# A written-out order for every engine, and a different first batch, in an attention and gated feed-forward kernel

## The chip, the cores and the metric

The kernel runs on one core of one Trainium2 chip. The metric is the device time of one execution in microseconds (us). Most executions of one kernel agree within 0.3 to 1%; a run more than 1.5% above the fastest of its kernel is called slow, and ratios use the other, fast, runs alone. "Span" is the length of the one execution that the profiler recorded; it is some 2 us shorter than that execution's device time. The engines are PE (TensorE, matmuls; PEld is its weight load), DVE (VectorE), ACT (ScalarE), POOL (GpSimd) and SP (SyncE, which here only issues transfers).

## The reference

```python
# x: (4, 12416, 128), inducing: (32, 128), w_gate, w_val: (128, 1536), w_out: (1536, 128); all fp32
def mab(q, kv):
    s = scale * (q @ kv.transpose(0, 2, 1))
    s = s - s.max(-1, keepdims=True)
    a = np.exp(s)
    a /= a.sum(-1, keepdims=True) + 1e-09
    return a @ kv
h = mab(I, x)                       # 32 inducing points look at the 12416 tokens of a batch
return mab(x, h)                    # the tokens look at the 32 results
...
gate = 1.0 / (1.0 + np.exp(-(x @ w_gate)))
val = x @ w_val
return (gate * val @ w_out)         # on all 49664 tokens
```

`h` of a batch needs all of that batch, and every output of the batch needs `h`. So before the first output there is a **prologue** (all of batch 0 loaded, cast, transposed, scored and summed); later batches do this beside the outputs of the batch ahead of them.

## The kernel before

Each batch has 97 tiles of 128 tokens: six quads of 16 tiles, the last with a 17th. A **unit** is 512 tokens; a batch has 24 and a tail of one tile, 24.25 in all. As the attention output is a weighted sum of 32 rows of `h`, the kernel folds `h` into the weights (`hw` is `h @ [w_gate w_val]`, 32 rows), so gate and value of a token are products of its 32 attention weights with `hw`. Matmuls write into the PSUM memory, where buffers are few. Per unit there are six gate products (PSUM buffer `g`, two of them), six tanh on ACT (sigmoid is 0.5 + 0.5 tanh(x/2)), twelve value products (PSUM buffer `v`, three), eleven of which DVE multiplies with the gate, one of which ACT copies out for GpSimd to multiply, 48 output matmuls into `acc`, and one copy of `acc` to SBUF by ACT.

```python
# one gate pair, one value block and its multiply (cut)
o = op("PE", 0.216, key + 0.1 + 0.05 * k, gd + ([g0] if g0 else []), mode="R", rg=k,
       need=[] if g0 else ["G"], emit=em, name=f"G{b}.{u}.{lo}.{k}")
a = act(w, key, gs + tg.old, give=[(g0, "G")], name=f"T{b}.{u}.{lo}",
        emit=lambda o, g0=g0, tg=tg, w=w: ACT.activation(out=tg.t[:, 0:w], in_=psl("G", g0)[:, 0:w], func=AF.Tanh, scale=0.5))
...
key = 1000 + LEAD + m // 2 + (0.05 if m % 2 == 0 else 0.3)
v = op("PE", 0.216, key, gd, mode="R", rg=rg, need=["V"], emit=em, name=f"V{b}.{u}.{q}")
d = dve(512, key, [v, a] + ub.old, give=[(v, "V")], name=f"D{b}.{u}.{q}",
        emit=lambda o, v=v, tg=tg, t0=t0, ub=ub: DVE.scalar_tensor_tensor(
            out=ub.t[:], in0=tg.t[:, t0 : t0 + TOK], scalar=1.0, in1=psl("V", v)[:], op0=ALU.add, op1=ALU.mult))
```

The operations carry a key, a duration, their dependences and the PSUM buffer that they need or give back. A list scheduler orders them while the program is built: each engine takes, among its pending operations in the order of the keys, the one that is ready first.

```python
def schedule(ops, pools, window=120):
    ...
    pend = {e: sorted((o for o in ops if o.eng == e), key=lambda o: o.key) for e in engs}
    ...
            for o in pend[e][: (60 if e in ("SP", "POOL") else window)]:
                ...
                r = max(r, d.start if d.eng == e == "PE" else d.end + (d.tail if d.eng != e or e in ("SP", "POOL") else 0.0))
                ...
                if cand is None or r < cand[0] - 1e-9:
                    cand = (r, o)
```

On the chip that order is then fixed: each engine executes its own list from first to last and waits at an entry whose inputs or buffers are not there, even if a later entry could go. The prologue loads the inducing points first, through GpSimd's own queue, then x through three staging buffers, and casts half of each quad on DVE and half on GpSimd; ACT casts two of the weights.

```python
ind_ld = op("POOL", 0.9, -10, tail=2.0, emit=lambda o: POOL.dma_start(ind16[:], inducing), name="ld ind")
...
c0 = op("DVE", 8 * P / 960 * 0.6 + 0.065, key + 3, [lm] + buf.old, name=f"cast{i}a",
        emit=lambda o: DVE.tensor_copy(out=buf.t[:, 0:h, :], in_=sg.t[:, 0:h, :]))
c1 = op("POOL", 8 * P / 960 + 0.3, key + 3, [lm] + buf.old, name=f"cast{i}b",
        emit=lambda o: POOL.tensor_copy(out=buf.t[:, h:QS, :], in_=sg.t[:, h:QS, :]))
...
wl["wo"] = op("POOL", 3.0, 40, [landed(ld, max(0.1, arrive[0] - 0.6 * 9))], name="wo2", ...)   # out weights times 0.5
```

The softmax here doesn't subtract the row's maximum and nothing guards it: scores larger than these inputs give would overflow.

Of the kernel before, what the change touches and what calls it, by code (L numbers as in the profile page):

```python
# [18 lines left out]
SEM = 0.085  # L19
DRAIN = 0.166  # L20
SWITCH = 0.1
RSTEP = 0.005
TSTEP = 1.12
LEAD = 3


class Op:


    def __init__(self, eng, dur, key, deps=(), mode="F", rg=0, tail=0.0, need=(), give=(), emit=None, name=""):  # L30
        self.eng, self.dur, self.key = eng, dur, key
        self.deps = [d for d in deps if d is not None]
        self.mode, self.rg, self.tail = mode, rg, tail
        self.need, self.give, self.emit, self.name = list(need), list(give), emit, name
        self.start = self.end = None
        self.slot = None
        self.strict = False


def schedule(ops, pools, window=120):  # L40
    engs = sorted({o.eng for o in ops})
    pend = {e: sorted((o for o in ops if o.eng == e), key=lambda o: o.key) for e in engs}
    free = {e: 0.0 for e in engs}
    mode, rgb, peend = None, [0.0] * 4, 0.0
    slotfree = {p: {i: 0.0 for i in range(n)} for p, n in pools.items()}
    inf = 1e18
    order = []
    while len(order) < len(ops):
        best = None
        for e in engs:  # L50
            cand, t0 = None, free[e]
            stop = False
            for o in pend[e][: (60 if e in ("SP", "POOL") else window)]:
                if stop:
                    break
                stop = o.strict
                r = t0
                for d in o.deps:
                    if d.start is None:
                        r = inf  # L60
                        break
                    r = max(r, d.start if d.eng == e == "PE" else d.end + (d.tail if d.eng != e or e in ("SP", "POOL") else 0.0))
                if r >= inf:
                    continue
                for p in o.need:
                    r = max(r, min(slotfree[p].values()))
                if r >= inf:
                    continue
                if e == "PE":
                    if o.mode == "R":  # L70
                        r = max(r, rgb[o.rg]) if mode == "R" else max(r, peend + SWITCH)
                    else:
                        r = max(r, peend + (SWITCH if mode != o.mode else 0.0))
                if cand is None or r < cand[0] - 1e-9:
                    cand = (r, o)
                if r <= t0 + 1e-9:
                    break
            if cand and (best is None or cand[0] < best[0]):
                best = (cand[0], e, cand[1])
        if best is None:  # L80
            raise RuntimeError("no op can go: " + str({e: [o.name for o in pend[e][:3]] for e in engs}))
        r, e, o = best
        o.start, o.end = r, r + o.dur
        if e == "PE":
            if o.mode == "R":
                if mode != "R":
                    rgb = [0.0] * 4
                rgb[o.rg] = o.end
                free[e] = r + RSTEP
            else:  # L90
                free[e] = o.end
            peend = max(peend, o.end)
            mode = o.mode
        else:
            free[e] = o.end
        pend[e].remove(o)
        order.append(o)
        for p in o.need:
            i = min(slotfree[p], key=lambda k: slotfree[p][k])
            slotfree[p][i] = inf  # L100
            o.slot = i
        for s, p in o.give:
            slotfree[p][s.slot] = o.end + o.tail
    order.sort(key=lambda o: o.start)
    return order
# [13 lines left out]


class Buf:
    def __init__(self, t, old, users):
        self.t, self.old, self.users = t, old, users
# [10 lines left out]
def kernel(  # L134
# [19 lines left out]
    psum = ctx.enter_context(tc.tile_pool(name="ps", bufs=1, space=bass.MemoryType.PSUM))  # L154

# [9 lines left out]
    PSG = [ps(f"g{i}", [P, 2 * TOK]) for i in range(2)]  # L165
    PSV = [ps(f"v{i}", [P, TOK]) for i in range(3)]
    PSA = [ps("acc", [P, TOK])]
    POOLS = {"G": 2, "V": 3, "A": 1}
# [3 lines left out]
    ones = sb("ones", [P, P], F32)  # L172
    ind16 = sb("ind16", [M, C])
# [21 lines left out]
    N4 = [sb(f"n4{r}", [P, 4, 4, M]) for r in range(4)]  # L195
    A2PR = ring("a2p", 2, [P, 640])
    A2R = ring("a2r", 3, [P, 4, 640])
    dram = ctx.enter_context(tc.tile_pool(name="dr", bufs=1, space=bass.MemoryType.DRAM))
    DRR = Ring([dram.tile([P, 640], F16, name=f"dr{i}", tag=f"dr{i}") for i in range(3)])
    TGA = sb("tga", [P, 12 * 2 * TOK])  # L200
    TGR = Ring([TGA[:, 2 * TOK * i : 2 * TOK * (i + 1)] for i in range(12)])
    UR = ring("u", 18, [P, TOK])
    VSR = ring("vs", 2, [P, TOK], F32)
    PTR = ring("pt", 2, [P, TOK], F32)
    OSR = ring("os", 4, [P, 4, C], F32)

    XS = xT[1][:].bitcast(F32)
    XSR = Ring([XS[:, QS * P * i : QS * P * (i + 1)].rearrange("p (s c) -> p s c", c=P) for i in range(3)])
    XS1 = sb("xs1", [P, C], F32)
    WS = [TGA[:].bitcast(F32)[:, F * (1 + i) : F * (2 + i)] for i in range(3)]  # L210
# [3 lines left out]
    def chain(ins, eng):  # L214
        prev = last.get(eng)
        if prev is not None:
            tc.add_manual_dep(
                ins.ins,
                prev.name,
                mybir.DependencyInfo(mybir.DependencyClass.NoSync, mybir.DependencyReason.DATA),  # L220
                reason="order",
            )
        last[eng] = ins.ins
        return ins

    class Eng:
# [3 lines left out]
        def __getattr__(self, f):  # L230
            fn = getattr(self.e, f)

            def go(*a, **k):
                return chain(fn(*a, **k), self.name)  # L234

            return go
# [5 lines left out]
    _affine_eye(nc, ident[:], [[-1, P]])  # L242
    for r in range(4):
        _affine_eye(nc, I4[32 * r : 32 * r + 32, :], [[-1, M]])
    nc.vector.memset(ones[:], 1.0)
    for q in range(2):
        nc.vector.memset(sacc[q][:], 0.0)
        nc.gpsimd.memset(ER.tiles[q][:], 0.0)
# [3 lines left out]
    def op(eng, dur, key, deps=(), **k):  # L252
        tails = {"PE": DRAIN + SEM, "ACT": 0.12 + SEM, "DVE": 0.085 + SEM, "POOL": 0.25, "SP": 2.6}
        k.setdefault("tail", tails[eng])
        o = Op(eng, dur, key, deps, **k)
        ops.append(o)
        return o

    def act(n, key, deps=(), **k):
        return op("ACT", n * 0.857e-3 + 0.03, key, deps, **k)  # L260

    def dve(n, key, deps=(), **k):
        return op("DVE", n / 960 + 0.065, key, deps, **k)

    def psl(kind, o):
        return {"G": PSG, "V": PSV, "A": PSA}[kind][o.slot]

    xv = [x[b].rearrange("(p s) c -> p s c", p=P) for b in range(B)]
    ov = [out[b * N : (b + 1) * N].rearrange("(p s) c -> p s c", p=P) for b in range(B)]


    units = [(b, u) for b in range(B) for u in range(NB + 1)]
    gfirst, vfirst, wsteps, gap = {}, {}, {}, {}
    ng = nv = 0
    lastw = -10
    for b, u in units:
        gfirst[b, u] = ng
        vfirst[b, u] = LEAD + nv / 2
        ng += 2 if u == NB else 6
        nv += 3 if u == NB else 12  # L280
        st = max(int(vfirst[b, u]) + 3, lastw + 2)
        ws = [st] * 12 if u == NB else [st, st, st + 1, st + 1, st + 1, st + 2, st + 2, st + 3, st + 3, st + 3, st + 4, st + 4]
        wsteps[b, u] = ws
        lastw = ws[-1]
        gap[b, u] = lastw + 1

    steps = {}

    def at_step(n):

        n = min(max(int(n), 0), ng - 1)
        return [steps[n]] if n in steps else []


    wl = {}
    ind_ld = op("POOL", 0.9, -10, tail=2.0, emit=lambda o: POOL.dma_start(ind16[:], inducing), name="ld ind")
    ind_t = op("PE", 0.1, -9, [ind_ld], need=["V"], name="indT",
               emit=lambda o: PE.transpose(psl("V", o)[:].bitcast(F16)[:, 0:M], ind16[:], ident[0:M, 0:M]))
    ind_c = dve(32, -9, [ind_t], give=[(ind_t, "V")], name="indTc",
                emit=lambda o: DVE.tensor_copy(out=indT[:], in_=psl("V", ind_t)[:].bitcast(F16)[:, 0:M]))  # L300
    BW = 330e3
    xload = {}

    def load_quad(b, i, key, after=()):
        buf = XR.take()
        ns = QS + 1 if i == NQ - 1 else QS
        o = op("POOL", 0.6, key, list(buf.old) + list(after), tail=8.0, name=f"ld x{b}.{i}",
               emit=lambda o: POOL.dma_start(buf.t[:, 0:ns, :], xv[b][:, i * QS : i * QS + ns, :]))
# [525 lines left out]
```

## Time and profile before

| | before |
|---|---|
| median of its first three runs (range) | 778.87 us (776.96 to 779.79) |
| first gate matmul, first output copied out of `acc` | 53.5 us, 67.6 us |
| from output 5 to 30, 30 to 55, 55 to 80 (a batch each, 24.25 units) | 183.1, 181.0, 182.3 us |
| from output 80 to 98 (18 units, nothing of a next batch beside them) | 124.7 us |

### The profile page before, as it was taken

To read this page: it belongs to the slowest core of one execution; us is meant where nothing else is said; L and a number is where in the kernel's file an instruction comes from. 1 tells how busy PE (TensorE), PEld (TensorE's weight loads), DVE (VectorE), ACT (ScalarE), POOL (GpSimd) and SP (SyncE) were. 2 spreads that over 40 slices of the span, in tenths; PEclk is the share of its full clock that TensorE was granted. 3 is DMA by queue.
4 is the path that set the end of the run, shared out by engine and by line. 5 is a ranking of instruction groups with operands and counts; after the bars stand their busy time and mean duration, and the time that the engine had idled before them with its cause. 6 is when DMAs were issued, how large, how long until landed. Compare 5 with 4: busy or idle time off the path is not lost.

```text
span 778.2 us, 20470 instructions
## 1 busy us (share of the span) xinstructions
PE 684.4 (88%) x7851; PEld 369.7 (48%) x7851; DVE 692.4 (89%) x1157; ACT 698.7 (90%) x883; POOL 339.2 (44%) x448
## 2 busy tenths in 40 slices
PE   3579988899899988989899988999989999999997
PEld 2324544445454544545445444444545454445444
DVE  2548998999899999999899999999899999999997
ACT  2449998999999999999899999999899989999996
POOL 3424453534525445445444436344354445445332
PEclk9758999999999999999999999999999999999999
DMA  9772449565421329675422236522231213222211
GB/s 349 184 124 67 108 88 180 116 129 132 95 73 53 90 82 158 130 164 115 122 70 66 69 96 118 124 71 77 60 104 36 79 64 74 81 72 59 79 43 45
DMA packets 113186, 78.64 MB, mean 101 GB/s; under 512 B 80576, under 2 KB 97472, under 8 KB 112320
## 3 DMA queue, kind: packets, MB, share of 16 engines
q1 hardware_dynamic: 110448, 67.80, 32.8%
q0 software_dynamic: 2640, 9.54, 7.9%
q8 instruction: 61, 1.00, 0.6%
q14 instruction: 37, 0.30, 0.1%
HBM read 39.99 MB, written 28.57 MB: 88 GB/s over the span
## 4 chain that ended last, share of the span: by engine, by line
PE 50%; issue 16%; POOL 12%; ACT 10%; DVE 9%; DMA 2%; ACTq 0%; POOLq 0%; DVEq 0%
PE acc L234 26%; PE v L234 20%; DVE u L234 7%; ACT tga L234 6%; POOL u L234 4%; POOL pt L234 4%; PE g L234 4%; ACT os L234 2%; POOL tree L234 2%; POOL a2n L234 2%; DMA a<-eT 2%; DVE x L234 1%; DMA ind<-in_inducing_dram 1%; ACT xT L234 1%; ACT eT L234 0%
## 5 line engine op out<-in xcount | busy, mean ns | idle before, releaser
L234 DVE SCALAR_TENSOR_TENSOR u<-tga,v 128x512 f16<-128x512 f16 x1068 | 663.4, 682 | 44.7 <-PE v L234 32.0
L234 ACT ACTIVATE tga<-g 128x1024 f16<-128x1024 f32 x584 | 579.8, 1039 | 31.9 <-PE v L234 8.1
L234 PE MATMUL v<-a2r,hw 32*128 32x512 f16 (+1 forms) x1200 | 338.9, 379 | 21.0 <-DVE u L234 20.6
L234 PEld LDWEIGHTS <-u 128*128 128x128 f16 x4656 | 266.4, 99 | 183.0 <-issue 181.7
L234 PE MATMUL acc<-wo,u 128*128 128x128 f16 x4656 | 349.9, 222 | 0.7 <-ACT os L234 0.7
L234 POOL TENSOR_TENSOR pt<-tga,vs 128x512 f32<-128x512 f16 x96 | 111.8, 1164 | 354.3 <-ACT vs L234 346.9
L234 PE MATMUL g<-a2r,hw 32*128 32x512 f16 (+1 forms) x1200 | 230.2, 383 | 32.7 <-ACT tga L234 32.0
L234 PEld LDWEIGHTS <-hw 32*128 32x128 f16 x2400 | 70.4, 91 | 139.6 <-issue 87.0
L234 POOL TENSOR_TENSOR u<-pt,vs 128x512 f16<-128x512 f32 x96 | 121.7, 1267 | 7.6
L234 ACT COPY vs<-v 128x512 f32<-128x512 f32 x96 | 56.5, 588 | 8.4 <-PE v L234 7.3
L234 ACT COPY os<-acc 128x512 f32<-128x512 f32 (+1 forms) x100 | 58.2, 582 | 3.3 <-PE acc L234 3.3
L234 POOL TENSOR_TENSOR a2n<-e2t,rc 128x128 f16<-128x128 f16 x96 | 37.3, 481 | 18.4 <-DVE rc L234 18.4
L234 ACT COPY xT<-v 128x1024 f16<-128x1024 f16 (+1 forms) x7 | 6.3, 906 | 23.1 <-PE v L234 23.1
L234 POOL TENSOR_TENSOR tree<-tree 128x64 f32<-128x64 f32 (+4 forms) x69 | 23.7, 344 | 5.4
L234 POOL DMA_DIRECT2D x<-in_x_dram x18 | 10.5, 585 | 27.6 <-PE v L234 13.4
L234 ACT ACTIVATE e<-g 128x512 f16<-128x512 f32 (+1 forms) x24 | 15.5, 649 | 4.3 <-PE g L234 4.3
L234 ACT ACTIVATE eT<-g 128x512 f16<-128x512 f32 (+1 forms) x28 | 15.6, 563 | 3.2 <-PE g L234 3.2
L234 PE MATMUL g<-xT,indT 128*32 128x512 f16 (+1 forms) x112 | 13.2, 388 | 3.9 <-ACT xT L234 2.9
L234 PEld LDWEIGHTS <-hT 128*32 128x32 f16 (+1 forms) x136 | 6.5, 95 | 20.4 <-issue 18.2
L234 PEld LDWEIGHTS <-a 128*32 128x32 f16 x388 | 7.3, 98 | 18.6 <-issue 9.5
L234 POOL TENSOR_TENSOR tree<-e2t 128x256 f32<-128x256 f16 (+1 forms) x23 | 15.9, 690 | 0.4 <-DMA e2t<-e 0.4
L234 PE MATMUL v<-ident,x 128*128 128x128 f16 x97 | 10.5, 281 | 3.9 <-DVE x L234 2.4
(59 smaller groups left out, 141.5 us busy)
## 6 DMA issues: line engine op xcount, KB each, us to landing
out_dram<-os SPq DMA_DIRECT2D x96, 256.0 KB, 2.0
a2r<-dr SPq DMA_DIRECT2D x92, 128.0 KB, 2.8
x<-in_x_dram POOLq DMA_DIRECT2D x15, 512.0 KB, 5.7
xT<-in_x_dram SPq DMA_DIRECT2D x6, 1024.0 KB, 9.0
dr<-a2p SPq DMA_DIRECT2D x19, 128.0 KB, 2.0
x<-in_x_dram POOLq DMA_DIRECT2D x3, 544.0 KB, 5.3
xT<-x SPq DMA_TRANSPOSE x75, 2.5
tga<-in_moe_w_gate_dram SPq DMA_DIRECT2D x1, 768.0 KB, 10.3
```

Of the source, the lines that this page charges most:

```text
L234: return chain(fn(*a, **k), self.name)
```

## The change

Its intent is to take the order out of the scheduler's hands: the order of all five engines for the whole program is written down, 5,627 names, and the build only plays it. With it came a different first batch: six fp32 loads at once into buffers that are idle then, casts on GpSimd, the last quad's scores token-major in three parts, summed straight into the accumulator.

```diff
-LEAD = 3
+COPIES = (3,)
+ORDER = {
+    "PE": """
+        xt0.8 xt0.0 indT xt1.8 sa0.0 xt1.0 ap0 xt2.8 sa0.1 xt2.0 hp0.0 ap1 xt3.0 sa0.2 hp0.1 xt3.8 ap2 xt4.0 hp0.2 sa0.3
...   (PE, ACT, DVE, POOL: some 390 lines of names cut)
+    "SP": """
+        lx0.0 lx1.0 lx2.0 lx3.0 lx4.0 lx5.8 lx5.0 lx5.13 lwg lind lwo lwv xd1.0.2 xd1.0.0 xd1.0.3 xd1.0.1 et0.1 xd1.1.0
...
-def schedule(ops, pools, window=120):
-    engs = sorted({o.eng for o in ops})
-    pend = {e: sorted((o for o in ops if o.eng == e), key=lambda o: o.key) for e in engs}
...
+def play(ops, order, pools):
+    by = {o.name: o for o in ops}
+    todo = {e: [by[n] for n in names] for e, names in order.items()}
...
+                    o.slot = len(u) % n          # PSUM buffers are taken in turn
...
-    ind_ld = op("POOL", 0.9, -10, tail=2.0, emit=lambda o: POOL.dma_start(ind16[:], inducing), name="ld ind")
+    ld = load(ind32[:], inducing, 40000, "lind")                     # by SP's queue, tenth in its order
+    ind_b = dve(64, [ld], "ind16", lambda o: DVE.tensor_copy(out=ind16[:], in_=ind32[:]))
...
-    XSR = Ring([XS[:, QS * P * i : QS * P * (i + 1)].rearrange("p (s c) -> p s c", c=P) for i in range(3)])
+    XS = [f32v(TGA)[:, 0 : QS * P]] + [f32v(xT[1])[:, QS * P * i : QS * P * (i + 1)] for i in range(3)]
+    XS += [f32v(UA)[:, 0 : QS * P], f32v(UA)[:, QS * P : (2 * QS + 1) * P]]
...
+    for i in range(NQ - 1):
+        load0(i, ((0, QS, ((0, 8, "POOL"), (8, 16, "POOL"))),))
+        xt_pe(i, ((0, 8), (8, 16)))
+        stage1_pro(i)
+    i = NQ - 1
+    load0(i, ((0, 8, ((0, 4, "POOL"), (4, 8, "DVE"))), (8, 13, ((8, 10, "POOL"), (10, 13, "DVE"))),
+              (13, 17, ((13, 15, "DVE"), (15, 17, "ACT")))))
+    groups = ((0, 8), (8, 13), (13, 17))
+    stage1_last(i, groups, xt_pe(i, groups))
...
-        wl[nm] = act(F, 25 + n, ..., name=nm, emit=lambda o, n=n, dst=dst: ACT.copy(out=dst, in_=WS[n]))
+        wl[nm] = op("POOL", 1.7, [ld], nm, lambda o, n=n, dst=dst: POOL.tensor_copy(out=dst, in_=WS[n]))
```

The counts of tanh, products, copies and output matmuls of a unit stay. In the names, `lx`/`cx` load and cast x of batch 0, `lind` and `lwg lwv lwo` load inducing points and weights, `G T V D C P W E` are gate matmuls, tanh, value matmuls, DVE products, ACT copies, GpSimd products, output matmuls and the copy of `acc`; `ld` and `xd` load and transpose x of later batches, `sa` is a first score, `et tr mu` the row sums of second scores.

## The prediction

> **What bounds the kernel now.** I read the page's shares and slices first, then a table by stage, then the timeline of the first 60 us, then the waits of the long middle.
>
> The page's first part gives busy time by engine:
>
> ```profile
> PE 684.4 (88%) x7851; PEld 369.7 (48%) x7851; DVE 692.4 (89%) x1157; ACT 698.7 (90%) x883; POOL 339.2 (44%) x448
> ```
>
> Three engines stand within 14 us of each other, so there is no single bound, and freeing one of them is worth little. The table by stage tells more (columns: stretch, its length, then busy us of PE, PEld, DVE, ACT and POOL with counts, granted clock, DMA share, GB/s):
>
> ```profile
> 80.00:700.00 620.00, 563.00 (x6546) 303.71 (x6546) 577.96 (x970) 587.25 (x740) 280.28 (x367) 0.99 0.41 96
> 700.00:765.00 65.00, 60.48 (x680) 31.84 (x679) 63.92 (x106) 62.66 (x76) 25.90 (x28) 1.00 0.18 58
> ```
>
> From 80 to 700 us ACT is busy 94.7% and DVE 93.2%; from 700, where no work for a next batch is mixed in, DVE reaches 98.3%. Of one unit (512 tokens, 12 column blocks) ACT does six tanh, one copy of v and one copy of the output. DVE does eleven products. In runs without a gap a tanh starts every 0.92 us (a pair took 1.94, one alone 1.02), a copy every 0.49, a product every 0.60. So a unit asks 6 x 0.92 + 2 x 0.49 = 6.5 us of ACT and 11 x 0.60 = 6.6 of DVE. A batch adds about 10.4 us of ACT: six first scores at about 0.7, six second ones at 0.55, three folds at 0.92. Over 24 units that is 0.43, so 6.93 for ACT. What is achieved: from 100 to 700 the view of the tanh alone counts 489, which is 81.5 units, 7.36 us each; in the three busier batches (100 to 600: 404 tanh) it is 7.43. In the last batch the copies of v stand 6.85 us apart. So the loss against the floor is about 0.5 us a unit in three batches, and about 0.25 in the last.
>
> What ended the gaps there (waits from 80 to 765 us: total us, times, longest):
>
> ```profile
> PE g L234 <- ACT tga L234: 31.1, 51, 0.7
> DVE u L234 <- PE v L234: 27.3, 79, 1.3
> PE v L234 <- DVE u L234: 23.7, 103, 1.1
> ```
>
> PE waits for a g buffer that ACT empties, DVE for a v, PE for a v buffer that DVE empties: a ring of three busy engines around two g and three v buffers. Only order can mend that, not a cheaper instruction.
>
> The prologue, from the timeline (start, length, engine, what, idle time before it and who ended it):
>
> ```profile
> 3.98 0.71 POOL L234 DMA_DIRECT2D ind<-in_inducing_dram  x1
> ...
> 9.78 0.20 PE L234 MATMUL v<-ident,ind 32*128 32x32 f16 x1 [9.78 <-DMA ind<-in_inducing_dram]
> ...
> 24.36 6.36 DVE L234 CAST x<-xT 128x1024 f16<-128x1024 f32 x1
> ...
> 45.15 0.29 DVE L234 TENSOR_TENSOR hT<-v,rsb 128x128 f16<-128x128 f32 x1
> ...
> 53.50 1.03 PE L234 MATMUL g<-a2r,hw 32*128 32x512 f16 x4 [0.52 <-DVE a2r L234]
> ```
>
> The inducing points arrive at 9.8, one DVE cast takes 6.36 us instead of its usual 0.68, the first h is ready at 45.4, the first gate matmul is at 53.5. That is 7% of the span with ACT mostly idle.
>
> **What the Trainium skill says.** (1) "DMA: Bandwidth & Descriptors", section "Two DMAs through the same engine are not ordered": within one queue of one engine, descriptors start in order. The trace agrees. The DMA issues of the first 60 us:
>
> ```profile
> tga<-in_moe_w_gate_dram SPq DMA_DIRECT2D x1, 768.0 KB, 10.3
> tga<-in_moe_w_val_dram SPq DMA_DIRECT2D x1, 768.0 KB, 11.5
> xs<-in_x_dram SPq DMA_DIRECT2D x1, 64.0 KB, 9.1
> ```
>
> The 64 KB load, issued at 2.1 behind three loads of 1 MB, landed only at 11.2, just after the third of those (whose cast starts at 11.09); the weights at 13.1 and 15.0. (2) "SBUF — State Buffer", section "Who interferes with whom": a DVE copy in a two-port mode and a GpSimd instruction shut each other out. The 6.36 us cast agrees: GpSimd had two casts and the scaling of wo (4.12 us) running from 24.04 to 30.16. (3) "TensorE: Matmul & The Clock Gate", Part 1: the clock halves when the engine has been idle and returns after some 3.4 us of activity. The trace agrees: eight transposes took 1.03 us when cold at 14.4, sixteen took 1.07 from 18.2.
>
> **The change part by part.**
>
> Prologue. *Removed:* the waits of loads four to six for a staging buffer, DVE's half of the casts for five quads, the ACT casts of the weights (2 x 1.48), the expansion copies on GpSimd. *Added:* casts on GpSimd (1.04 per half quad), token-major scores for the last quad (17 small matmuls, and 34 more that sum straight into the accumulator). Loads land 2.5 us apart (casts began at 6.03, 8.53, 11.09), so x would be in by about 19 us, and compute could follow closely.
>
> But the written order has a flaw. The inducing points now go by the SP queue, behind all of x (6.36 MB) and the gate weight (0.79 MB), and their cast is the first instruction of DVE; their transpose is PE's third. At 2.5 us per MB after a first landing at 6.0: x is in at 18.8, the gate weight at 20.7, the inducing points at about **21 us**. DVE and PE stand still until then; before, they started at 9.8. From 21 I walked the written orders with durations of before. Four stored casts are waiting, PE becomes warm after about 4 us, and each quad costs PE 16 transposes (1.1), scores (0.5), a transpose of the weights (0.35) and the product (0.4), 2.4 us and waits on ACT of about 0.7. Five quads so take until about 36.5; the last one's score, base matmuls in fp32 (1.1) and 34 sums (2.0) bring h to about 41 (45.4 before). Then small scores, exponent, sum, reciprocal, product, transposes, copy: about 6.3 us (8.1 before), mixed with the folds. First gate matmul at about **47.2 instead of 53.5: 6.3 us won**. Were the inducing points in time, everything would start at 7 and the gain would be some 20 us.
>
> Middle. Counts of tanh, copies, products and output matmuls are unchanged; the copied block moves from 1 to 3; buffers are now taken in turn. PE's bursts number 621 row-mode ones in the written text, 6.4 a unit, against about 6 in the trace, so PE neither gains nor loses. What can be won is only the 0.5 us a unit of the first three batches and 0.25 of the last: 73 x 0.5 + 24 x 0.25 = 42 us as a limit. A fixed order by a finer model of delays should win some of it, not most: real semaphores and DMA do not keep to it, and a wrong guess on one engine stalls the others. I take 0.2 a unit in three batches and 0.05 in the last, 73 x 0.2 + 24 x 0.05 = 15.8 us.
>
> End. The last tanh to the end of the span is 7 us before, and the order ends with the same two evacuations: nothing. Sum: 778.9 - 6.3 - 15.8 = 756.8, so **757 us**.
>
> **The rivals.** *A: the inducing points are not late* (small transfers pass, or arrive over idle engines). For it: before, they took only 5.8 us beside full traffic. Against: that was GpSimd's own queue; the 64 KB load in the SP queue did wait. Then some 743. *B: the order gives nothing in the middle.* For it: in the last batch DVE is at 98% already, and the old order was tuned too. Then 772. *C: the order turns slack into new waits:* the chain through SP (transposes, write, replication) lies in a fixed order of about 500 transfers, and a late one stops PE at its next gate matmul; before, PE waited for such transfers only 3.6 us in the middle. With 0.1 us a unit lost it would be 782. *D: the order reaches 98% of the ACT floor:* 30 us won in the middle, 742.
>
> **Range and chances.** Late points with 5 to 27 us from the middle give 746 to 768; the prologue may be off by 4; A and D pull down. I take 742 to 770. The 2% line is at 763.3, 6 above my figure. Chances: faster 0.73, same 0.25, slower 0.02.
>
> **What would show it.** Right if the new trace has DVE's first cast and PE's third group at about 21 us with the inducing load as releaser, h at 41, the first gate matmul at 46 to 49, and 7.1 to 7.3 us a unit in the first three batches with ACT over 96% busy. Wrong in the prologue if PE is at work by 10 us, or cold throughout (matmuls of 0.6 us instead of 0.39), or if DVE is again shut out by GpSimd's weight casts near 40. Wrong in the middle if a unit takes 7.4 or more, with PE or DVE waiting for transfers or for GpSimd, or under 7.0.

## More of the kernel before

The outputs are counted in the timeline by ACT's copies `os<-acc`; the difference of two such starts is the pace of the whole machine, whichever engine sets it.

From the page of the kernel before, the clock row (one digit for each fortieth of the span, 9 is full) and the two largest groups of DVE and ACT (count | busy us, mean ns | idle just before them, and what ended most of it):

```profile
PEclk9758999999999999999999999999999999999999
...
L234 DVE SCALAR_TENSOR_TENSOR u<-tga,v 128x512 f16<-128x512 f16 x1068 | 663.4, 682 | 44.7 <-PE v L234 32.0
L234 ACT ACTIVATE tga<-g 128x1024 f16<-128x1024 f32 x584 | 579.8, 1039 | 31.9 <-PE v L234 8.1
```

The clock is down for the second, third and fourth slice, which is the prologue. DVE's products and ACT's tanh fill those engines, and each still has over 30 us of idle time in front of them. Of DVE's 44.7 us PE's `v` ended 32.0; ACT's 31.9 have several causes, of which PE's `v` is the largest with 8.1. PE in turn waits for both: the middle is a ring of three engines, each nearly full, none of them alone the bound.

## The result

The changed kernel took 737.41 us (median of 4 runs, 733.21 to 739.23), the kernel before in the same rounds 778.55. The ratio is 0.9465, 95% interval 0.942 to 0.951: faster, by 5.4% (4.9 to 5.8). All ratios here are the mean time of one kernel's fast runs over the mean of the other's fast runs in the same rounds, so not quite the ratio of the medians. The time lies 4.6 us below the predicted range.

From the page of the changed kernel, the shares, the clock row and the same two groups; its span was 731.4 us, at the fast end of its runs:

```profile
PE 679.9 (93%) x7928; PEld 381.4 (52%) x7928; DVE 677.7 (93%) x1156; ACT 681.0 (93%) x881; POOL 342.6 (47%) x452
...
PEclk9958999999999999999999999999999999999999
...
L626 DVE SCALAR_TENSOR_TENSOR ua<-tga,v 128x512 f16<-128x512 f16 x1056 | 648.5, 681 | 18.7 <-PE g L626 7.5
L626 ACT ACTIVATE tga<-g 128x1024 f16<-128x1024 f32 x576 | 562.4, 1078 | 5.1 <-PE v L626 1.8
```

The idle time in front of the tanh fell from 31.9 to 5.1 us and in front of the products from 44.7 to 18.7. Then the table by stage for 80 to 700 us (length; busy us and counts of PE, PEld, DVE, ACT, POOL; granted clock, DMA share, GB/s):

```profile
80.00:700.00 620.00, 604.19 (x6998) 337.26 (x6996) 612.66 (x1040) 616.77 (x793) 297.23 (x387) 1.00 0.44 102
```

ACT is busy 99.5% and DVE 98.8% of this stretch. The waits from 60 to 715 us (us in total, times, longest):

```profile
PE v L626 <- DVE ua L626: 9.4, 41, 0.5
...
DVE ua L626 <- PE v L626: 4.0, 12, 0.9
...
PE g L626 <- ACT tga L626: 1.6, 7, 0.4
```

These were 23.7, 27.3 and 31.1 us before, in a window 30 us longer (80 to 765): most of the ring's waits have gone. The starts of the output copies say the same:

| us | before | after | difference |
|---|---|---|---|
| start to first output | 67.6 | 67.9 | +0.3 |
| output 1 to 5 | 29.6 | 30.3 | +0.7 |
| three batches (5 to 80) | 546.4 | 503.7 | -42.7 |
| output 80 to 98 | 124.7 | 119.9 | -4.8 |
| output 98 to the end of the span | 9.9 | 9.6 | -0.3 |
| span | 778.2 | 731.4 | -46.8 |

**Everything was won in the middle, and the new prologue won nothing up to the first output.** A unit of the first three batches takes 503.7 / 72.75 = 6.92 us, against 7.51 before. The timeline of the changed prologue (start, length, engine, what, idle before it and who ended that):

```profile
20.90 0.21 DVE L626 CAST ind<-ind 32x128 f16<-32x128 f32 x1 [19.73 <-DMA ind<-in_inducing_dram]
...
36.89 0.29 DVE L626 TENSOR_TENSOR hT<-acc,rsb 128x128 f16<-128x128 f32 x1
...
38.55 4.12 POOL L626 TENSOR_SCALAR wo<-hw 128x1536 f16<-128x1536 f32 x1
...
39.13 3.09 DVE L626 TENSOR_TENSOR nb<-eb,rb 128x384 f16<-128x384 f16 x1
...
44.70 0.61 PE L626 MATMUL g<-a2r,hw 32*128 32x512 f16 x2 [0.53 <-DVE a2r L626]
...
54.27 0.61 PE L626 MATMUL g<-xT,indT 128*32 128x512 f16 x3 [5.03 <-DMA xT<-x]
```

DVE's first instruction after its memsets waits until 20.9 for the inducing points; `h` is ready at 37.2 and the first gate matmul goes at 44.7, 8.8 us earlier than before. Then it is lost again. GpSimd's scaling of the output weights runs beside a DVE product that takes 3.09 us, and the first score of batch 1 stands in PE's order ahead of most gate work and waits 5.03 us for transposes. The transfers, first of 0 to 60 and then of 30 to 60 us (size, us from issue to landing):

```profile
ind<-in_inducing_dram SPq DMA_DIRECT2D x1, 16.0 KB, 12.7
```

```profile
x<-in_x_dram POOLq DMA_DIRECT2D x4, 512.0 KB, 9.0
xT<-x SPq DMA_TRANSPOSE x8, 9.0
```

In the same window of the kernel before, with three such loads and 16 transposes, a transpose took 2.5 us to land and a load of x 5.5.

### The profile page after: what moved, and what is told of

It reads as the page before. It is cut to its first block, busy times and chain, and to the rows that moved or that the text cites. A ratio compares the mean times of both kernels' runs of the same rounds, so it can differ in the third digit from the quotient of the medians.

```text
span 731.4 us, 20034 instructions
## 1 busy us (share of the span) xinstructions
PE 679.9 (93%) x7928; PEld 381.4 (52%) x7928; DVE 677.7 (93%) x1156; ACT 681.0 (93%) x881; POOL 342.6 (47%) x452
## 4 chain that ended last, share of the span: by engine, by line
PE 50%; DVE 20%; ACT 15%; DMA 6%; issue 6%; POOL 2%; SPq 1%; ACTq 0%; POOLq 0%; DVEq 0%
PE acc L626 24%; DVE ua L626 19%; PE v L626 17%; ACT tga L626 12%; PE g L626 8%; DMA ind<-in_inducing_dram 2%; DMA xT<-x 2%; ACT os L626 2%; DMA out_dram<-os 1%; ACT vs L626 1%; SPq L626 1%; DMA xT<-in_x_dram 1%; POOL pt L626 1%; POOL ua L626 1%; ACT eT L626 0%
## 5 line engine op out<-in xcount | busy, mean ns | idle before, releaser
L626 DVE SCALAR_TENSOR_TENSOR ua<-tga,v 128x512 f16<-128x512 f16 x1056 | 648.5, 681 | 18.7 <-PE g L626 7.5
L626 ACT ACTIVATE tga<-g 128x1024 f16<-128x1024 f32 x576 | 562.4, 1078 | 5.1 <-PE v L626 1.8
L626 PE MATMUL acc<-wo,ua 128*128 128x128 f16 x4608 | 360.6, 221 | 2.0 <-DVE ua L626 0.3
L626 PEld LDWEIGHTS <-ua 128*128 128x128 f16 x4608 | 261.8, 98 | 172.6 <-issue 162.7
L626 PE MATMUL v<-a2r,hw 32*128 32x512 f16 (+1 forms) x1200 | 329.2, 376 | 12.5 <-DVE ua L626 10.0
L626 PEld LDWEIGHTS <-hw 32*128 32x128 f16 x2400 | 89.5, 91 | 116.4 <-issue 49.3
L626 POOL TENSOR_TENSOR ua<-pt,vs 128x512 f16<-128x512 f32 x96 | 121.7, 1268 | 7.5
L626 ACT COPY os<-acc 128x512 f32<-128x512 f32 (+1 forms) x100 | 62.3, 623 | 7.1 <-PE acc L626 6.7
L626 POOL TENSOR_TENSOR a2n<-e2t,rc 128x128 f16<-128x128 f16 x96 | 37.2, 484 | 18.3 <-DVE rc L626 17.5
L626 POOL TENSOR_TENSOR tree<-e2t 128x256 f32<-128x256 f16 (+1 forms) x23 | 15.8, 687 | 24.2 <-DMA e2t<-e 24.2
L626 POOL TENSOR_TENSOR tree<-tree 128x64 f32<-128x64 f32 (+4 forms) x69 | 23.7, 344 | 5.4
L626 ACT CAST hw<-g 128x1024 f16<-128x1024 f32 x11 | 11.7, 1076 | 0.8 <-PE g L626 0.7
L626 PEld LDWEIGHTS <-x 128*128 128x128 f16 x114 | 7.9, 113 | 8.6 <-POOL x L626 7.1
```

The costliest lines, as they stand in the source:

```text
L626: ins = fn(*a, **k)
```

## The experiments

Twelve runs of eleven kernels (e10 is e8 again) were made, each timed against the kernel before in the same rounds (its median there 778.07 to 779.69). "First output" and the batches are from one profiled run each.

| kernel | median (range), us | ratio, 95% interval | first gate matmul | first output | three batches |
|---|---|---|---|---|---|
| after | 737.41 (733.21 to 739.23) | 0.9465 (0.942 to 0.951) | 44.7 | 67.9 | 168.1, 168.2, 167.4 |
| e1 | 721.84 (718.99 to 724.65) | 0.9283 (0.9246 to 0.932) | 35.0 | 54.7 | 168.1, 168.5, 167.4 |
| e2 | 777.38 (776.4 to 781.61) | 1.0008 (0.997 to 1.0047) | 45.7 | 64.6 | 184.3, 182.8, 179.8 |
| e3 | 817.7 (812.57 to 822.89) | 1.0539 (1.0477 to 1.0601) | 45.8 | 72.0 | 187.1, 181.7, 187.6 |
| e4 | 736.73 (736.52 to 737.32) | 0.9476 (0.945 to 0.9502) | 46.5 | 66.0 | 168.1, 167.8, 168.8 |
| e5 | 769.32 (765.55 to 770.69) | 0.986 (0.9832 to 0.9889) | 44.9 | 75.5 | 178.0, 176.5, 173.5 |
| e6 | 778.59 (773.1 to 782.65) | 0.9982 (0.9929 to 1.0036) | 45.0 | 70.4 | 174.4, 176.5, 178.0 |
| e7 | 725.15 (722.05 to 730.63) | 0.9317 (0.9267 to 0.9366) | 32.5 | 58.2 | 168.3, 168.2, 167.4 |
| e8 | 720.87 (716.88 to 732.14) | 0.923 (0.9179 to 0.928) | 34.4 | 60.2 | 170.8, 167.8, 167.4 |
| e10 (e8 again) | 722.8 (717.82 to 723.43) | 0.9274 (0.9249 to 0.9299) | 31.3 | 54.4 | 168.4, 167.8, 168.7 |
| e9 | 723.22 (716.61 to 726.61) | 0.9272 (0.9233 to 0.931) | 32.9 | 52.9 | 170.8, 168.2, 167.4 |
| e11 | 716.82 (715.72 to 721.66) | 0.9231 (0.9204 to 0.9259) | 32.9 | 50.2 | 168.4, 168.2, 167.4 |
| e12 | 721.73 (715.02 to 726.19) | 0.9263 (0.9226 to 0.93) | 34.7 | 58.2 | 168.4, 168.0, 167.4 |

### What made the middle faster: e2, e3, e5, e6

**e2** keeps everything of the change but the order, and with it the copied block, from the gate stage on, which are those of the kernel before.

```diff
-COPIES = (3,)
+COPIES = (1,)
 ORDER = {
-    "PE": """ ... G0.0.0 V0.0.2 G0.0.1 ...          (from the gate stage on, all engines)
+    "PE": """ ... the sequence that the list scheduler of the kernel before gives, in the new names
```

> The changed kernel with its prologue, buffers and operations, but after the prologue every engine has the order of the kernel before (copied block 1 as there). Theory (the written order alone made the middle faster): a batch takes 180 to 184 us from evacuation to evacuation again, instead of 167.9, and the time is 770 to 785. Rival (buffers taken in turn, own buffers for the short unit, one operation for both halves of g): a batch stays at 168 to 172 and the time at 733 to 745.

Measured: 777.38 us, and batches of 184.3, 182.8 and 179.8 us. The ring's waits (80 to 765 us) are back near those of the kernel before (31.1, 27.3, 23.7):

```profile
PE g L660 <- ACT tga L660: 30.1, 48, 0.7
DVE ua L660 <- PE v L660: 24.1, 76, 1.0
PE v L660 <- DVE ua L660: 23.3, 99, 1.1
```

So the buffers in turn, the tail's own buffers and the joint gate operation are worth nothing by themselves that the total shows, and neither is the prologue with its late inducing points: **the written order, with its copied block, is the gain.** The order and the copied block (3 instead of 1) changed together here, and no run parts them.

**e3** asks whether PE's order alone carries it. PE, GpSimd and SP keep the written order; ACT and DVE take their operations in the order in which a play of the kernel's own durations makes them ready. Mostly neighbours swap places.

```diff
 ORDER = {
-    "ACT": """ ... the written order
-    "DVE": """ ... the written order
+    "ACT": """ ... first ready, first placed
+    "DVE": """ ... first ready, first placed
```

> The changed kernel, but ACT and DVE take their operations in the order in which a planning model says they are ready, which differs from the written order by small swaps (an evacuation after instead of before a tanh, two neighbouring products exchanged). PE, GpSimd and SP keep the written order. Theory A (PE's order carries the gain, neighbours on the other engines do not matter): 735 to 742, 168 to 170 us a batch. Theory B (the gain needs the exact order of all engines together): 755 to 785, 174 us a batch or more, with ACT and PE waiting for each other.

It took 817.7 us, worse than the kernel before and than the range expected. Its waits from 80 to 765 us:

```profile
DVE ua L657 <- PE v L657: 29.3, 56, 1.2
PE v L657 <- DVE ua L657: 25.6, 66, 1.6
...
ACT tga L657 <- PE g L657: 23.7, 42, 1.6
```

**e5 and e6** do this on one engine alone (in e5 365 places of DVE change, in e6 78 of ACT).

> The written order of every engine is kept except that of the vector engine, whose operations go in the order in which a play of the written durations makes them ready (365 of its places change, nearly all swaps of neighbours). e3 changed this and the scalar engine's order together and cost 80 us. Theory A (the loss comes from either engine alone, since a late multiply holds back the same buffers as a late activation): about half of e3's loss or more, 765 to 795 us. Theory B (only the two together hurt, because one engine in the written order pulls the other back into step): 737 to 750 us.

> The same with the scalar engine alone (78 places change), the vector engine as written. Theory A: 755 to 795 us though far fewer places change. Theory B: 737 to 750 us.

Measured 769.32 and 778.59 us. Waits of 80 to 740 us, of e5 and of e6:

```profile
PE v L657 <- DVE ua L657: 25.7, 68, 1.6
DVE ua L657 <- PE v L657: 13.1, 30, 0.9
```

```profile
PE v L657 <- ACT vs L657: 18.7, 23, 1.8
DVE ua L657 <- PE v L657: 17.9, 36, 1.7
```

Either swap alone gives back most (e5) or all (e6) of the change's gain. Per batch e5 loses 8.1 us on average and e6 8.4, their sum 16.5, and e3, with both, 17.6. So Theory B of e5, that an engine in the written order pulls the other back into step, fell. That the losses add up is a hint: it is one profile each, and e3 changed a few more places (376 and 83). In e6, 78 places on ACT suffice: PE now waits 18.7 us for the copies of `v` on ACT, which hold one of three `v` buffers.

The clock, too, differs between these runs. The table by stage for 80 to 700 us, of e3 and of e6 (the clock is the third number from the end; the change has 1.00 there):

```profile
80.00:700.00 620.00, 573.25 (x6371) 314.67 (x6370) 563.99 (x943) 569.91 (x722) 272.61 (x359) 0.96 0.40 95
```

```profile
80.00:700.00 620.00, 586.05 (x6648) 325.62 (x6645) 583.86 (x985) 589.86 (x754) 283.78 (x375) 0.97 0.42 98
```

From output 5 to 80 the clock was at half for 13.7 us in e5, 27.3 in e6 and 47.8 in e3, for 17.1 in the kernel before and never in the change. PE can lose at most half of such time. So, as an estimate, the clock accounts for at most 6.8 of the 24.4 us that e5 loses there, 13.7 of e6's 25.2 and 23.9 of e3's 52.7, and for at most 8.5 of the 42.7 us that the change won. Whether the waits brought the clock down, or the clock the waits, was not tried. Another limit of these three: "ready first" is by the durations written in the kernel, not by the chip, so they show that small swaps are dear, and not what another careful order would give.

### What the prologue lost: e1, e4

**e1** moves one name: the load of the inducing points goes to the head of SP's order.

```diff
     "SP": """
-        lx0.0 lx1.0 lx2.0 lx3.0 lx4.0 lx5.8 lx5.0 lx5.13 lwg lind lwo lwv
+        lind lx0.0 lx1.0 lx2.0 lx3.0 lx4.0 lx5.8 lx5.0 lx5.13 lwg lwo lwv
```

> The changed kernel with one edit: the load of the inducing points goes first in the SP queue instead of tenth. Theory (late points cost the whole delay): they land by 5 us instead of 20.9, so PE and DVE go on at 7 instead of 21, h comes 10 to 13 us earlier (at about 25 instead of 37) and the time falls to 724 to 728. Rival (the prologue is bound by transfers anyway): loads and transposes for the second batch fill the DMA engines until about 57 us, the first score of the second batch waits for them as before, and the first output still is evacuated near 65 to 68 us; then the time stays within 734 to 740.

It took 721.84 us, 15.6 less than the change as it came and 2 below the expected range; `h` came at 26.1 (37.2 before). The 16 KB now land 1.6 us after issue instead of 12.7 (transfers of 0 to 30 us):

```profile
ind<-in_inducing_dram SPq DMA_DIRECT2D x1, 16.0 KB, 1.6
```

The first output comes 13.2 us earlier and the middle is unchanged. The timeline shows what is left: PE waits for the value weights, whose load is still the last of the weights in the queue, and the first gate matmul goes at 35.0.

```profile
29.96 0.59 PE L657 MATMUL g<-wv,hT 128*128 128x512 f16 x1 [2.83 <-POOL wv L657]
...
35.02 0.61 PE L657 MATMUL g<-a2r,hw 32*128 32x512 f16 x2 [0.53 <-DVE a2r L657]
```

**e4** keeps the late inducing points and clears the wait for the transposes instead: three of the loads of batch 1 go later on GpSimd, and two transposes that follow a score (`at1.0`, `bt0.1`) go ahead of transposes of x in SP's order.

```diff
     "POOL": ld1.0 wg wv wo tr0.1 ld1.1 mu0.1 ld1.2 P0.0.3 ld1.3     (was ld1.0 ld1.1 wg ld1.2 wv wo ld1.3 tr0.1 mu0.1 P0.0.3)
     "SP":   et0.1 at1.0 bt0.1 xd1.1.0 xd1.1.2 ...                    (was et0.1 xd1.1.0 xd1.1.2 xd1.2.3 at1.0 xd1.2.2 bt0.1)
```

> The changed kernel with the second, third and fourth x load of the second batch moved behind the first sum tree on GpSimd, and on SP the first two transposes that follow a score put ahead of the transposes of those loads. Theory (the stop of PE from 49.2 to 54.3 us is a jam of transfers: four x loads and eight transposes at once): the first score of the second batch no longer waits, PE's 5.0 us wait is gone, the first output is evacuated 4 to 7 us earlier than 67.9, time 731 to 734. Rival (the transposes are slow by themselves): the wait stays at 3 us or more and the time at 736 to 740.

The wait for transposes went, and the time stayed at 736.73 us: neither expectation holds. Two losses took its place. The timeline shows the first:

```profile
32.57 5.06 DVE L657 TENSOR_SCALAR ssb<-ones,ssum 128x128 f32<-128x128 f32 x1
...
33.42 4.12 POOL L657 TENSOR_SCALAR wo<-hw 128x1536 f16<-128x1536 f32 x1
...
37.71 0.62 PE L657 MATMUL acc<-x,a 128*32 128x128 f16 x16 [4.49 <-DVE a L657]
```

With the loads out of the way GpSimd runs its three weight operations back to back from 30.6 to 37.5, and DVE's small multiplication, 0.28 us elsewhere, takes 5.06; PE waits 4.49 us behind it. The second is in the table by stage, from 52 to 78 us (the last three numbers are clock, DMA share and GB/s):

```profile
52.00:78.00 26.00, 25.58 (x192) 11.37 (x192) 17.31 (x30) 19.93 (x24) 11.32 (x17) 0.50 0.93 146
```

PE is busy 25.58 of 26 us at half clock. From output 1 to 5 e4 takes 36.6 us, against 30.3 in the changed kernel.

### Why an earlier first gate matmul stopped paying: e7 to e12

**e7** adds to e1 an earlier load of the value weights, and moves the halving of the output weights from GpSimd to DVE.

```diff
     "SP":   lind ... lx5.13 lwg lwv lwo                  (was lwg lwo lwv)
     "POOL": ... wv ld1.3 tr0.1                           (wo taken out)
     "DVE":  ... rcp0 wo D0.0.2                           (wo put in)
-    wl["wo"] = op("POOL", 2.3, [ld], "wo", lambda o: POOL.tensor_scalar(
+    wl["wo"] = op("DVE", 1.7, [ld], "wo", lambda o: DVE.tensor_scalar(
```

> e1 (inducing points loaded first) plus the two losses that its trace still shows ahead of the first gate matmul (35.0 us): the load of the value weights goes ahead of that of the output weights, and the halving cast of the output weights goes from GpSimd, where it took 4.12 us and shut the vector engine out, to the vector engine's gap after the last row copy of the prologue. Theory: first gate matmul near 32 us, and as the first score of batch 1 still waits in the tensor engine's order for the transposes of its rows, that wait grows from 1.6 us to 3 to 5 us; total 717 to 722 us against 721.8 of e1. Rival (the loads of batch 1 set everything from here on): 721 to 724 us.

The first gate matmul did come at 32.5, the product that had taken 3.09 us beside GpSimd took 0.54, and the halving 0.96 us on DVE instead of 4.12 on GpSimd. But the output weights now landed late and DVE's list stood still for them:

```profile
28.22 0.54 DVE L657 TENSOR_TENSOR nb<-eb,rb 128x384 f16<-128x384 f16 x1
...
38.90 0.96 DVE L657 TENSOR_SCALAR wo<-hw 128x1536 f16<-128x1536 f32 x1 [6.43 <-DMA hw<-in_moe_w_out_dram]
```

It took 725.15 us, above both expected ranges: no gain over e1.

**e8** also writes the first score of batch 1 four gate matmuls later, on PE and on ACT.

```diff
     "PE":  ... V0.0.9 V0.0.0 G0.0.2 ... W0.0.0 V0.1.0 sa1.0 G0.2.0      (was V0.0.9 sa1.0 V0.0.0)
     "ACT": ... T0.0.5 T0.0.2 ... T0.1.0 xsa1.0 T0.2.0                   (was T0.0.5 xsa1.0 T0.0.2)
```

> e7 with the first score of batch 1 written four gate matmuls later on the tensor engine, and its exponential as much later on the scalar engine. Theory: the wait for the transposes goes, the first output leaves 3 us or more earlier than in e1 (below 52 us), total 714 to 719 us. Rival (its late exponential holds back the sums of batch 1, or the row sums of quad 1 become the next wait): within 2 us of e7.

Four times between 716.88 and 732.14 us and a slow profile; so it ran once more as **e10**.

> e8 once more, unchanged, since its profile fell in the slow state and its four times lay between 717 and 732 us. If those times were the state's and not the kernel's: a fast profile with a first output near 57 us and a median of 716 to 719 us. If its prologue differs from run to run by where the transfers collide: again a spread of some 8 us among fast runs.

Median 722.8 us, a first output at 54.4 us and a spread of 5.6: neither e8 nor e10 differs from e1 beyond the spread, and e10's median lies above the 714 to 719 us expected of e8. The two profiles of this one kernel differ in the stretch of 52 to 78 us, of e8 (slow) and e10 (fast):

```profile
52.00:78.00 26.00, 25.68 (x185) 12.03 (x183) 17.74 (x29) 18.72 (x22) 12.91 (x19) 0.51 0.39 80
```

```profile
52.00:78.00 26.00, 24.96 (x282) 13.32 (x281) 24.82 (x42) 25.41 (x34) 13.00 (x18) 1.00 0.57 106
```

In one PE is busy for 25.68 us at 0.51 of its clock and does 185 groups of matmuls, in the other it does 282 at full clock. **e9** tries the transfers, setting the loads of batch 1 further apart.

```diff
     "POOL": ... ld1.0 wg wv ld1.1 tr0.1 ld1.2 mu0.1 ld1.3 P0.0.3        (on top of e8)
     "SP":   ... et0.1 at1.0 xd1.1.0 xd1.1.2 bt0.1 xd1.2.3 ...
```

> e8 with the loads of batch 1 set apart: the second right after the weight casts, the third and fourth among the row sums of the first scores, and the load queue takes the transposes that batch 0 waits for ahead of those of the later quads. Theory (what is left of the prologue is the transfers of batch 1 in the way of the transposes): the row sums of the second quad start before 44 us instead of 48, the first output leaves near 52 us, total 709 to 716 us. Rival (the later loads come too late for the scores of batch 1, which then make the gate stage wait): 717 to 728 us.

The first output came at 52.9 as expected, the time did not: 723.22 us, with a spread of 10. From output 1 to 5 it takes 35.8 us. Its granted clock fell at 36 us and came back at 70. **e11** is e9 with eight useless matmuls of 512 columns in PE's waits of 33 to 36 us; **e12** puts them into e8.

```diff
+    def warm(n, k):
+        def em(o):
+            for _ in range(k):
+                PE.matmul(ACC[:, 0:TOK], lhsT=ident[:], rhs=wg[:, 0:TOK], start=True, stop=True, skip_group_check=True)
+        op("PE", 0.22 * k, [hTd[0], wl["wg"]], f"wm{n}", em)
+    for n, k in enumerate((3, 3, 2)):
+        warm(n, k)
     "PE": ... V0.0.8 wm0 G0.0.4 wm1 G0.0.5 wm2 V0.0.9 ...
```

> e9 with eight useless matmuls of 512 columns (into the accumulator that is free there) in three of the tensor engine's waits between the first gate matmuls, 33 to 36 us, so that it does not look idle. In e9's profile the granted clock fell to one half at 36 us and came back only at 70 us, with the tensor engine busy all of that time, and from the first to the fifth output it took 35.8 us against 30.3 in e1. Theory (the halved clock, called forth by these waits, eats what the earlier first gate matmul won): no half clock after 36 us or a far shorter one, 30 to 31 us from the first to the fifth output, total 713 to 719 us. Rival (the clock falls anyway, or the multiplies are what sets the pace): 720 to 726 us as e9.

> The same eight matmuls in e8, whose two profiles had the half clock from 37 to 76 us (span 730.3, slow) and from 35 to 52 us (720.5). Theory: at most a short half clock, a smaller spread among the runs than the 8 to 15 us of e8, median 713 to 719 us. Rival: 720 to 724 us with the same spread.

e11 took 716.82 us, in the expected range, five of its six runs within 3.1 us. The table by stage from 36 to 70 us, of e9 and of e11:

```profile
36.00:70.00 34.00, 33.31 (x239) 14.64 (x239) 23.53 (x40) 26.97 (x33) 16.45 (x28) 0.50 0.63 109
```

```profile
36.00:70.00 34.00, 31.19 (x316) 14.77 (x316) 29.62 (x51) 32.01 (x43) 19.00 (x30) 0.95 0.68 113
```

The clock goes from 0.50 to 0.95, and DVE's and ACT's busy time in these 34 us from 23.5 and 27.0 to 29.6 and 32.0. The spans of the two profiles differ by 9.3 us: 2.7 had come by the first output, 4.3 come from output 1 to 5 (35.8 against 31.6), and 2.4 in the first batch, where e9's clock fell once more (0.88 and 0.69 from 204 to 220 us, 1.00 in e11). So in these two profiles the halved clock is what ate most of e9's gain; nothing ties the fall at 204 to 220 us to the eight matmuls. The medians are 6.4 us apart, but the two intervals overlap a little. **e12 shows nothing either way:** 721.73 us, slow profile; after the eight matmuls its PE stood nearly still again from 42 to 46 us (2.9 us of it for transposes), and the clock was at half from 46 to 66 us.

The record holds a check that needs no profile, since every run lists its mean granted clock. e9's six runs go from 716.61 us at 0.985 to 726.61 at 0.965; e11's are all at 0.982 or more. The change itself goes from 733.21 us at 0.984 to 739.23 at 0.965. Over the 60 runs of the change and its variants, each set against its own mean, the time rises by about 0.30 us for each us at half clock, as worked out from the mean clocks (correlation 0.91). e4 is an exception: its four runs lie within 0.8 us at clocks of 0.969 to 0.981. So much of the spread within one kernel goes with the clock.

e11 has the lowest median, 0.9231 of the time before. Its interval overlaps that of e1, which moves one name alone, so that it beats e1 is likely but not shown.

## Why the prediction was wrong

The direction and the first signs were right; the size was not: 22 us predicted, 41 measured between the medians, 46.8 between the profiled spans. Two misses pulled opposite ways: 31.7 us too little in the middle, and 7.3 too much up to output 5.

- **The failed step is the size of the middle term**: "A fixed order by a finer model of delays should win some of it, not most", "I take 0.2 a unit in three batches and 0.05 in the last", 15.8 us. Measured: 7.51 - 6.92 = 0.59 us a unit in three batches and 4.8 / 18 = 0.27 in the last, 47.5 us. A unit "under 7.0" was among its signs of being wrong in the middle, and came. The limit itself was right in kind: the floor of 6.93 us of ACT for a unit is what the change reaches (6.92), with ACT at 99.5%. It was a little low (42 us) because 7.43 a unit came from counting tanh, where the outputs give 7.51. Rival D, the floor reached, had the mechanism, at 30 us instead of 47. What I argued against it, that "a wrong guess on one engine stalls the others", e3, e5 and e6 show to be true of a careless order; the written one does not make those guesses.
- **The prologue term failed differently: right events, wrong end.** Late inducing points at "about 21 us": 20.9, and e1 shows them to cost 13.2 us to the first output, near the 13.7 between my 20 us without them and 6.3 with them. `h` at "about 41" came at 37.2 and the first gate matmul at 44.7 instead of 47.2. But "6.3 us won" took the first gate matmul for the end of the prologue. What counts is the first output, and there 0.3 us was lost. I had not followed the next things in the order past that point: the score of batch 1 behind four loads and their transposes, and a clock at half until 60 us. e7 to e11 show the same once more: up to 4 us gained at the first gate matmul gave nothing until the clock was held up.
- **The end: nothing**, as predicted (-0.3 us).
- Rival A (points not late), B (nothing in the middle) and C (new waits in the middle) fell, though C's late transposes did stop PE once, for 5.03 us in the prologue; B is what e2 measures, at 777.4 instead of the 772 that I gave it, because the prologue won 3.0 us at the first output there and not 6.3.
- "DVE again shut out by GpSimd's weight casts near 40" was named as a sign, and is there: 3.09 us against 0.54. What it costs by itself is not shown: in e7, where it is gone, DVE waits 6.43 us for the output weights instead.
- Of the skill's points, two held as used. "DMA: Bandwidth & Descriptors", section "Two DMAs through the same engine are not ordered" (descriptors of one queue start in order) fits the 12.7 us of the 16 KB. "SBUF — State Buffer", section "Who interferes with whom" (a two-input DVE product and a DVE operation in a two-port mode contend with GpSimd) fits 3.09 against 0.54 us and 5.06 against 0.28, though in which mode the second ran no view shows. The third did not: see the last section. The lines that I gave for it show two speeds, and not the 3.4 us; in that trace PE starts at 9.8 us and the full clock comes at 16.7.

What stays open: why the clock returns when it does. What the change's own 20 us at half clock cost it was not tried on the change itself; its four runs say only that time and clock go together. And whether any other careful order reaches the floor too; only the written one, the old one and three damaged ones ran.

## What to carry to other kernels

Where several engines are each over 90% busy around few PSUM buffers, work out the floor of the fullest one, and do not rule out that an explicit order for all engines reaches it, as it did here; then test how fragile it is, since swaps of neighbours on one engine took back most of the gain. Read the worth of a prologue at the first output and not at the first matmul of the next stage, and read each queue's order for a small load that stands behind large ones. When the tensor engine is busy without a gap in a stage and still slow, look at the granted clock before anything else, and compare runs at like clocks.

## What the Trainium skill lacked or had wrong

- "TensorE: Matmul & The Clock Gate", Part 1, says that the full clock returns after about 3.4 us of sustained activity. Here e9's PE was busy 33.31 of 34 us at 0.50 of its clock, and e4's 25.58 of 26; in ten profiles read in steps of 2 us, the stretch at half clock after the start of the gate stage lasted from some 3 us (e11) to some 40 (e8, slow). The page warns that clock events in a trace can be unreliable and stick; but the same groups of matmuls take 0.61 us in these stretches and 0.39 after them, and the outputs are late by 5 us, so the records are right. The step itself is in the traces: each stretch at half clock that lies whole within one of the fourteen profiles is a multiple of 3.41 us, from one (e11) to twelve (e8, 41.0 us). What fails is that one busy step is enough. The same kinds of matmuls run at full clock through the middle, so why it stays at half here is open. The measurement decides: do not plan with one step.
- The same page says that the half clock comes after at least one idle window of about 3.4 us. Here less was enough: in e9 three waits of PE, 1.8 us in all between 33.5 and 36.1 us, came just before it. In e11, where eight matmuls fill them, it came at 43.5 us and stayed for 3.4.
- "SBUF — State Buffer", section "Who interferes with whom", names who blocks whom and gives as sizes only "DVE 6.8× slower" and "GpSimd 1.5× slower". Here a DVE multiplication of 0.28 us took 5.06 beside GpSimd, 18 times as long. GpSimd's halving of 128x1536 fp32 took 4.12 us where DVE needed 0.96.
- No page that I read gives the landing time of a DMA transpose beside large loads: 2.5 us in the kernel before beside three loads of 512 KB, 9.0 us in the change beside four; e4, with the loads set apart, lost the wait.
